# A delta-rule attention and a softplus MLP in one hand-ordered program: one inverse for the first two chunks, its joins split, memsets moved, weights loaded earlier, the order redrawn

## The chip, the core and the metric

The kernel runs on one core of a Trainium2 chip. The time is the device time of one execution in microseconds (us); the figure for a kernel is the median of its runs. The engines are named as in the profile: PE (TensorE) multiplies matrices, with PEld its weight loads; DVE (VectorE) and POOL (GpSimd) work element by element; ACT (ScalarE) evaluates functions and copies; SP (SyncE) issues DMA transfers. Each engine takes its own instructions strictly in the order in which the program lists them.

## The reference, cut to what matters

Four sequences of 768 tokens, 8 heads, 48 features per head. A recurrent state of 48 x 48 per sequence and head is read by the query and corrected by the key; the result, scaled by g, goes through a two-layer MLP with softplus (384 to 2048 to 384) over all 3072 tokens.

```python
k_n = k / (np.linalg.norm(k, axis=-1, keepdims=True) + 1e-06)
for t in range(S):
    readout = np.einsum('bhd,bhde->bhe', q[:, :, t], state)
    y[:, :, t] = g[:, :, t] * readout
    v_old = np.einsum('bhde,bhd->bhe', state, kt)
    state = state + bt[:, :, :, None] * np.einsum('bhd,bhe->bhde', kt, vt - v_old)
...
h = x @ w_in
g = np.maximum(h, 0.0) + np.log1p(np.exp(-np.abs(h)))
return (g @ w_out).astype(np.float32)
```

## The kernel before, in words

**Chunks.** The 768 steps are cut into 12 chunks of 64. Inside a chunk the recurrence becomes a triangular system of 64 x 64 for each of the 32 pairs of sequence and head; between chunks only the state is carried. Chunks are taken in pairs, six in all.

**Front** (`front`, line 468). For one chunk: cast keys (kn) and queries (qn) to f16, transpose them on PE (8 products with the identity, line 485) into kqt by way of PSUM, with copies by ACT and DVE (lines 312 and 314 are the copy helper). The key gram (64 products, lines 522 and 527) gives the strictly triangular blocks kk, the query gram (32 products, line 561) gives mt after a multiplication with the mask (line 571). `norms` squares and sums the keys (lines 418 and 423) and takes the root: on ACT for the first two pairs, on POOL by a power (line 443) afterwards. `lane_beta` makes the factors bl.

**Inverse** (`inverse`, line 584). The blocks are transposed to ln (line 591, on DVE), scaled to nn (line 612), and a forward elimination of 15 steps, each a product (line 622) and a sum (line 629), inverts two 16 x 16 blocks per system, with all systems side by side in the lanes of tt. One pass always works on the shapes of two chunks, whether one chunk or two are in it. In the kernel before there are seven passes: one for chunk 0 on DVE, one for chunk 1 on POOL, and one for each of the other five pairs on POOL. The *join* that follows puts the small inverses together to those of 32 x 32 and 64 x 64: transposes of tt (lines 647 and 663, DVE), copies to f16 (lines 654 and 670, ACT), and three batches of PE products per chunk: xmm (64, line 684), tmm (68, lines 705 and 711) and zmm (34, lines 739 and 742), with evacuations between them, into td and z.

**Chain** (`chain`, line 765). For one chunk, in order: ks (line 786) from the state, w (line 829, or line 799 for chunk 0, which has no state), umm (line 840), u1, zu (line 877), u2, smm and the new state (lines 909 to 926), and beside it the output: qs, ymm (line 939), y times g (line 961), transposes ytr (line 979) into xt. For chunk 0 the products count 64 for umm, and 32 each for zu, smm and ymm, and 6 for ytr.

**Dense** (`dense`, line 998). Jobs of one chunk (the first two and the last two) or two chunks (the others): h = w_in x xt (g1, line 1014), softplus on ACT (line 1028), times w_out (g2, line 1044), evacuation to osb, store (line 1067). The first dense product needs chain 0 and w_in; the job of chunks 2 and 3 needs both of their chains.

**Order.** Nothing runs when it is called: every piece of work is an `Item` with an engine, a planned cost, what it depends on and the buffers it uses. `Plan.run` (line 86) simulates the engines with the planned costs and writes the instructions of each in the order that results; ties are broken by priorities. `_TABLE` (line 1108) gives, by position, the engine (of those that an item allows) and the priority of every item. The planner also has a model of PE's code supply: PE's products are counted in blocks of 128 (`BLOCK`), and a block is taken to arrive `FETCH` after the block before the last was begun.

**Loads.** SP issues k, q, v and g chunk by chunk, two DMAs of 192 KB each, as buffers come free (kf 3, qf 2, vf 4, gf 4). The eight weight loads (w_in and w_out in four parts each) are issued by POOL; each part waits on POOL's queue until a named load of SP has landed: before these are v0, q0, k2, k3 for w_in and q1, v1, g1, g1 for w_out. At the start POOL also issues beta's eight small DMAs, builds the mask, and clears kk, nv and tt (lines 272 and 275).

Of the kernel before, what the change touches and what calls it, by code (L numbers as in the profile page):

```python
# [10 lines left out]
F32 = mybir.dt.float32  # L11
# [34 lines left out]
class Plan:  # L46
# [3 lines left out]
    FETCH = 3.5  # L50
    HOP = 0.08
# [34 lines left out]
    def run(self):  # L86
# [3 lines left out]
        free = {e: 0.0 for e in left}  # L90
        pipe = 0.0
# [3 lines left out]
        while any(left.values()):  # L95
# [64 lines left out]
            if it.dma:  # L160
                free[e] = t0 + it.cost if e == "POOL" else max(t0 + it.cost, pipe - 4.0)
                pipe = max(pipe, t0 + it.cost) + it.dma
                it.end = pipe + 1.9
            elif e == "PE":
# [24 lines left out]
def kernel(  # L189
# [13 lines left out]
    P = 128  # L203
# [67 lines left out]
    def pool0(t):  # L271
        nc.gpsimd.memset(t, 0.0)
# [116 lines left out]
    weights(0, (("v", 0), ("q", 0), ("k", 2), ("k", 3)))  # L389
    weights(1, (("q", 1), ("v", 1), ("g", 1), ("g", 1)))  # L390
# [64 lines left out]
    def lane_beta(cc, nv, nv_it, prio):  # L455
# [9 lines left out]
        it = add("DVE", "lbeta", 0.8, fn, deps=[nv_it], bufs=[nv, nl, bl], prio=prio)  # L465
        return bl, it

    def front(c, kk, prio, late, en_k, en_q, en_kk):
# [9 lines left out]
        for j, x, x_it, pr in ((1, kn[c], kn_it[c], prio + 1), (0, qn[c], qn_it[c], prio + late + 1)):  # L478
# [33 lines left out]
            if j == 1:  # L512
                gk = [Buf(p_d), Buf(p_d)]

                def gram(gk=gk):
# [16 lines left out]
                    "PE", "gramk", 0.75, gram, deps=ev, bufs=gk + kq + [kk], prio=pr, mm=64,  # L532
# [17 lines left out]
            else:  # L550
# [3 lines left out]
                def gram(gm=gm):  # L554
# [9 lines left out]
                    "PE", "gramq", 0.45, gram, deps=its[0] + its[1], bufs=gm + kq + mt[c],  # L564
# [19 lines left out]
    def inverse(cs, kk, kk_it, bl, bl_it, on_dve, clear, prio, prio2):  # L584
# [51 lines left out]
        for j in range(15):  # L636
# [6 lines left out]
        u_all = slice(16 * cls[0], 16 * cls[-1] + 16)  # L643
        part = len(cs) / 2
# [6 lines left out]
        )  # L651
        e2 = add(
            "ACT", "tn", 0.17 + 0.92 * part,
            lambda: nc.scalar.copy(  # L654
                tn.ap[:, u_all], tn32.ap[:, :, u_all].rearrange("p j u -> p u j")
            ),
            deps=[e1], bufs=[tn32, tn], prio=prio2,
# [9 lines left out]
        l3 = add("DVE", "t32", 1.34, ttr, deps=[prev], bufs=[t32, tt], prio=prio2)  # L667
        l4 = add(
# [6 lines left out]

        xp, ep, xs, z = Buf(p_d), Buf(p_d), Buf(r_xs), Buf(r_z)
        e3, e5 = [], []
        for cl in cls:

            def xmm(cl=cl):  # L680
                for u in range(16 * cl, 16 * cl + 16):
# [8 lines left out]
                    "PE", "xmm", 0.53, xmm, deps=[e2], bufs=[kk, tn, xp, xs],  # L690
                    prio=prio2 + cl, mm=64, mode="3232",
# [7 lines left out]
        for cl in cls:  # L699

            def tmm(cl=cl):
# [7 lines left out]
                for u in range(16 * cl, 16 * cl + 16):  # L709
# [12 lines left out]
                    "PE", "tmm", 0.58, tmm, deps=[e4, l4], bufs=[xs, td, ep],  # L722
# [8 lines left out]
        for c in cs:  # L731
# [3 lines left out]
            def zmm(zp=zp, cl=cl):  # L735
# [13 lines left out]
                "PE", "zmm", 0.42, zmm, deps=[td_it], bufs=[kk, td, z, zp],  # L749
# [13 lines left out]
    xts, xt_it = {}, {}  # L763

    def chain(c, pr):
# [39 lines left out]
        else:  # L805

            def vscale():
# [14 lines left out]
                "PE", "ks", 0.37, lambda: with_state(C, wp, lambda b: {}),  # L822
# [13 lines left out]
        def umm(m):  # L836
            for pi in range(H):
# [13 lines left out]
                "PE", "umm", 0.31, lambda m=m: umm(m), deps=[a2[m], td_it],  # L851
# [12 lines left out]
        if not first:  # L864
            c0 = add(
                "PE", "qs", 0.37,
# [7 lines left out]
        def zu(m):  # L874
            for pi in range(H):
# [12 lines left out]
                "PE", "zu", 0.28, lambda m=m: zu(m), deps=[a4[m], z_it],  # L888
# [3 lines left out]
        ]  # L892
        a6 = [
# [6 lines left out]
        if not last:  # L900
# [3 lines left out]
            def smm(kn_=kn[c]):  # L904
# [11 lines left out]
                "PE", "smm", 0.37, smm, deps=a6, bufs=[kn[c]] + u2 + sp_ + s1, prio=pr,  # L916
# [35 lines left out]
        for m in range(2):  # L952
            c1 = add(
                "PE", "ymm", 0.3, lambda m=m: ymm(m), deps=[a6[m]] + mt_it[c],
# [43 lines left out]
    def dense(cs, pm):  # L998
# [8 lines left out]
        for f0 in range(0, NF, nb):  # L1007
            hp, gb = Buf(p_h), Buf(r_ga)

            def g1(f0=f0, hp=hp):  # L1010
# [12 lines left out]
                "PE", "g1", 0.655, g1, deps=[x for c in cs for x in xt_it[c]] + [wl[0][f0 // 4]],  # L1023
# [56 lines left out]
    for cc in range(1, NSS):  # L1080
# [4 lines left out]
        for c in cs:  # L1085
            kk_it += front(c, kk, pf, 70, "POOL", "POOL", ("ACT", "DVE"))
# [125 lines left out]
```

## Time and profile before

| | |
|---|---|
| median of 3 runs | 309.63 us (308.05 to 311.8) |
| profiled execution | 309.16 us |
| its span | 307.5 us |
| PE, DVE, ACT, POOL busy | 236.3, 158.9, 142.9, 142.6 us |
| instructions PE (products) | 6768 |
| DMA | 27.79 MB, of which PE's and the other engines' code 0.94 MB |
| mean granted clock of PE | 0.967 |

The span runs from the first to the last instruction that the profile shows; the time of the execution is a little longer. A row of the views by time gives the start, the length, the engine, the line, the operation and its tiles; "x8" is the number of instructions merged in a row. A row of the view by stretches gives, after the stretch and its length, each engine's busy us with its number of instructions, then PE's granted clock, the share of the DMA engines and GB/s. In the chain that ended last every piece is what the next piece waited for; "issue" is time in which an engine waited for nothing that the profile shows.

### The profile page before, as it was taken

Reading aid. Unit: us, or ns where it says so; the run is one execution under the profiler, and the core shown is the slowest. Engines: PE = TensorE matmul, PEld = TensorE weight load, DVE = VectorE, ACT = ScalarE, POOL = GpSimd, SP = SyncE. Lnnn points to the kernel's source line nnn. Section 1 sums busy time; section 2 is a strip of 40 time slices with the busy share of each in tenths; the row PEclk is TensorE's granted clock in tenths of the full one; section 3 lists DMA queues with packets and bytes.
Section 4 is the critical chain, followed back from the end, with each engine's and each line's share of the span. In section 5 each row is a group of like instructions: output and inputs, shape, how many; then the busy total and the mean of one; then the engine's idle time right before and its main releaser. Section 6 shows DMA issues by size and latency. Waiting matters only on the chain.

```text
span 307.5 us, 14779 instructions
## 1 busy us (share of the span) xinstructions
PE 236.3 (77%) x6768; PEld 155.8 (51%) x6768; DVE 158.9 (52%) x306; ACT 142.9 (46%) x240; POOL 142.6 (46%) x262
## 2 busy tenths in 40 slices
PE   0130183277988997899987999959999899999993
PEld 0120163255756765455664556636555555567761
DVE  1189998442757786854873474645436611152000
ACT  3070086022754656726654674352656516715531
POOL 8916578557138887457761747811087000000000
PEclk9999999999999999969997999987999979999999
DMA  8999439999015979699298430843000111021122
GB/s 115 158 179 173 57 54 191 186 170 152 7 31 100 157 140 158 113 162 148 51 164 147 83 57 15 125 99 79 6 5 15 43 28 30 2 55 28 27 53 51
DMA packets 107711, 27.79 MB, mean 90 GB/s; under 512 B 100865, under 2 KB 107649, under 8 KB 107649
## 3 DMA queue, kind: packets, MB, share of 16 engines
q1 hardware_dynamic: 103680, 23.60, 47.5%
q0 software_dynamic: 3968, 3.25, 7.1%
q8 instruction: 53, 0.87, 1.2%
q14 instruction: 10, 0.07, 0.1%
HBM read 25.26 MB, written 4.72 MB: 98 GB/s over the span
## 4 chain that ended last, share of the span: by engine, by line
PE 61%; DVE 12%; issue 11%; POOL 11%; ACT 4%; POOLq 0%; ACTq 0%
PE h L1014 19%; PE o L1044 18%; PE d L485 3%; POOL tt L629 3%; POOL tmp L622 3%; PE d L684 2%; PE d L786 2%; DVE tt L629 2%; PE d L840 2%; PE d L939 2%; DVE tmp L622 2%; PE d L711 2%; DVE ln L591 2%; PE d L561 2%; PE d L877 2%
## 5 line engine op out<-in xcount | busy, mean ns | idle before, releaser
L1044 PE MATMUL o<-w_out,ga 128*128 128x384 f16 x384 | 77.9, 343 | 3.2 <-issue 1.9
L1028 ACT ACTIVATE ga<-h 128x512 f16<-128x512 f32 x96 | 57.2, 599 | 48.0 <-PE h L1014 45.4
L1014 PE MATMUL h<-xt,w_in 128*128 128x512 f16 (+1 forms) x384 | 74.8, 336 | 1.0 <-issue 1.0
L1044 PEld LDWEIGHTS <-ga 128*128 128x128 f16 x384 | 35.7, 101 | 26.1 <-issue 7.3
L1014 PEld LDWEIGHTS <-w_in 128*128 128x128 f16 x384 | 36.1, 100 | 21.7 <-issue 3.4
L629 POOL TENSOR_TENSOR tt<-tt,tmp 128x30 f32<-128x30 f32 (+7 forms) x90 | 33.8, 375 | 7.0
L622 POOL TENSOR_TENSOR tmp<-nn,tt 128x30 f32<-128x30 f32 (+7 forms) x90 | 32.3, 359 | 6.4
L485 PE MATMUL d<-ident,kn 128*128 128x128 f16 x96 | 9.7, 258 | 30.8 <-POOL kn L314 28.3
L312 ACT ACTIVATE kqt<-d 128x512 f16<-128x512 f16 x26 | 15.0, 596 | 26.2 <-PE d L485 24.5
L314 DVE CAST u<-d 128x384 f16<-128x384 f32 x25 | 13.4, 552 | 26.3 <-PE d L877 18.5
L443 POOL TENSOR_TENSOR nv<-nv,half_c 128x32 f32<-128x32 f32 x4 | 22.0, 5509 | 7.4 <-DVE nv L423 7.4
L485 PEld LDWEIGHTS <-kn 128*128 128x128 f16 x96 | 7.1, 115 | 32.8 <-POOL kn L314 28.7
L571 DVE TENSOR_TENSOR mt<-d,mask 128x512 f16<-128x512 f32 x24 | 15.7, 683 | 9.9 <-PE d L561 9.8
L808 POOL TENSOR_TENSOR vf<-vf,nv 128x768 f32<-128x768 f32 x11 | 16.2, 1476 | 8.2 <-DMA vf<-in_v_dram 5.0
L314 DVE COPY osb<-o 128x384 f32<-128x384 f32 x12 | 6.6, 551 | 22.7 <-PE o L1044 22.7
L961 DVE TENSOR_TENSOR yg<-d,gf 128x384 f16<-128x384 f32 x24 | 12.8, 551 | 10.1 <-PE d L939 10.0
L654 ACT CAST tn<-tn 128x512 f16<-128x512 f32 (+1 forms) x7 | 6.7, 963 | 21.6 <-DVE tn L647 21.6
L314 DVE COPY kqt<-d 128x512 f16<-128x512 f16 x22 | 9.1, 422 | 14.6 <-ACT kqt L312 9.0
L423 DVE TENSOR_REDUCE nv<-ksq 128x16 f32<-128x768 f32 x12 | 11.4, 949 | 9.6 <-POOL nv L275 7.8
L312 ACT ACTIVATE u<-d 128x384 f16<-128x384 f32 x23 | 10.7, 490 | 10.7 <-PE d L840 7.4
L829 DVE TENSOR_TENSOR w<-vf,d 128x384 f16<-128x384 f32 x22 | 11.3, 547 | 8.2 <-PE d L786 4.5
L591 DVE STREAM_TRANSPOSE ln<-kk 128x1024 f16<-128x1024 f16 x7 | 13.3, 1905 | 4.2 <-ACT kk L312 4.0
(89 smaller groups left out, 379.4 us busy)
## 6 DMA issues: line engine op xcount, KB each, us to landing
kf<-in_k_dram SPq DMA_DIRECT2D x24, 192.0 KB, 5.4
vf<-in_v_dram SPq DMA_DIRECT2D x24, 192.0 KB, 5.5
qf<-in_q_dram SPq DMA_DIRECT2D x24, 192.0 KB, 5.5
gf<-in_g_dram SPq DMA_DIRECT2D x24, 192.0 KB, 5.3
out_dram<-osb SPq DMA_DIRECT2D x48, 96.0 KB, 2.3
w_in<-in_moe_w_in_dram POOLq DMA_DIRECT2D x4, 384.0 KB, 8.1
w_out<-in_moe_w_out_dram POOLq DMA_DIRECT2D x4, 384.0 KB, 8.6
beta_l<-in_beta_dram POOLq DMA_DIRECT2D x8, 12.0 KB, 4.5
```

Source lines behind the costliest of these rows:

```text
L312: nc.scalar.activation(o, x, AF.Copy, scale=float(sign))
L314: ENG[en].tensor_copy(o, x)
L443: lambda: nc.gpsimd.tensor_tensor(nv.ap[:, sl], nv.ap[:, sl], half_c[:, sl], ALU.pow),
L485: nc.tensor.transpose(o[:, NP * p + i], x.ap[:, p, 2 * i : 2 * i + 2].rearrange("p h d -> p (h d)"), ident,)
L571: nc.vector.tensor_tensor(o.ap, gm[m].ap.rearrange("p (n t) -> p n t", n=H), mask[:, None, :].broadcast_to([P, H, C]), ALU.mult,)
L591: lambda: nc.vector.transpose(ln.ap, kk.ap[:, 1].rearrange("p u t -> p t u")),
L622: eng.tensor_tensor(t, nn.ap[:, :, j + 1 :, j : j + 1].broadcast_to([P, 2, n, w]), tt.ap[:, :, j : j + 1, 16 : 16 + w].broadcast_to([P, 2, ...
L629: eng.tensor_tensor(rows, rows, t, ALU.add)
L808: nc.gpsimd.tensor_tensor(vf.ap, vf.ap, nv.ap[:, 16 * cl : 16 * cl + 16] .rearrange("p (a h) -> p a h", a=2)[:, :, :, None] .broadcast_to( ...
L1014: nc.tensor.matmul(hp.ap[:, n * b : n * b + n], w_in[:, j, f * P : (f + 1) * P], xt.ap[:, j, t0 : t0 + n], start=(j == 0), stop=(j == 2),)
L1028: lambda hp=hp, o=gb: nc.scalar.activation(o.ap, hp.ap, AF.Softplus),
L1044: nc.tensor.matmul(op.ap[:, :DM], b.ap[:, col + c0 : col + c0 + 128], w_out[:, f, :], start=(f == 0), stop=(f == NF - 1),)
```

## The change

- Chunks 0 and 1 are treated as a pair like the others: one inverse, on DVE. It waits for both chunks' kk and for norms over both.
- The join moves to a function of its own. For the first pair it is done chunk by chunk on the shared transposes: join of chunk 0, chain 0, join of chunk 1. On PE, xmm of chunk 1 is ordered behind zu of chain 0 (`hold`, `behind`).
- kk and nv are no longer cleared; tt is cleared at the start by DVE instead of POOL, and the clear within an inverse is left out for pair 1, which gets the second tt fresh.
- Loads: the order of the first ten becomes k0, k1, q0, v0, q1, k2, k3, g0, v1, g1. The four parts of w_in wait for k0, k0, k1, k1, those of w_out for g0, v1, g1, g1.
- The planner gets other costs for many items, a start time for each engine (`FREE`), a shorter `FETCH`, and an extra `BUSY` for code that is fetched while a weight load is under way.
- `_TABLE` is another one throughout.

The products of the key gram stay as they are; only their planned cost differs.

```diff
-    FETCH = 3.5
-    HOP = 0.08
+    FETCH = 3.2
+    BUSY = 2.3
+    HOP = 0.06
+    FREE = {"PE": 1.0, "ACT": 2.4, "DVE": 5.5, "POOL": 6.8, "SP": 0.8}
...
-                    arrive.append(end + self.FETCH)
+                    arrive.append(end + self.FETCH + (self.BUSY if end < wide else 0.0))
...
-    r_kk = ring("kk", 2, [P, 2, U, HC], F16, init=pool0)
-    r_nv = ring("nv", 3, [P, 32], F32, init=lambda t: nc.gpsimd.memset(t, 1.0))
-    r_t = ring("tt", 2, [P, 2, 16, 48], F32, init=pool0)
+    r_kk = ring("kk", 2, [P, 2, U, HC], F16)
+    r_nv = ring("nv", 3, [P, 32], F32)
+    r_t = ring("tt", 2, [P, 2, 16, 48], F32, init=lambda t: nc.vector.memset(t, 0.0))
...
-        ("k", k, r_k, 0), ("k", k, r_k, 1), ("v", v, r_v, 0), ("q", q, r_q, 0),
-        ("g", g, r_g, 0), ("k", k, r_k, 2), ("k", k, r_k, 3), ("q", q, r_q, 1),
+        ("k", k, r_k, 0), ("k", k, r_k, 1), ("q", q, r_q, 0), ("v", v, r_v, 0),
+        ("q", q, r_q, 1), ("k", k, r_k, 2), ("k", k, r_k, 3), ("g", g, r_g, 0),
...
-    weights(0, (("v", 0), ("q", 0), ("k", 2), ("k", 3)))
-    weights(1, (("q", 1), ("v", 1), ("g", 1), ("g", 1)))
+    weights(0, (("k", 0), ("k", 0), ("k", 1), ("k", 1)))
+    weights(1, (("g", 0), ("v", 1), ("g", 1), ("g", 1)))
...
-                    "PE", "gramk", 0.75, gram, deps=ev, bufs=gk + kq + [kk], prio=pr, mm=64,
+                    "PE", "gramk", 0.51, gram, deps=ev, bufs=gk + kq + [kk], prio=pr, mm=64,
...
+        l3 = add("DVE", "t32", 1.34, ttr, deps=[prev], bufs=[t32, tt], prio=prio2)
+        for grp in [[c] for c in cs] if apart else [cs]:
+            plan.tag = grp[0]
+            join(
+                grp, kk, tn32, e1, t32, l3, tn, td, xs, z,
+                prio2 + apart * (grp[0] - cs[0]), hold.get(grp[0] - 1, ()),
+            )
+            if apart and grp[0] == cs[0]:
+                chain(grp[0], -300)
+
+    def join(cs, kk, tn32, e1, t32, l3, tn, td, xs, z, prio2, behind):
...
-                    "PE", "xmm", 0.53, xmm, deps=[e2], bufs=[kk, tn, xp, xs],
-                    prio=prio2 + cl, mm=64, mode="3232",
+                    "PE", "xmm", 0.47, xmm, deps=[e2], bufs=[kk, tn, xp, xs],
+                    prio=prio2 + cl, mm=64, mode="3232", order=behind,
...
+        hold[c] = a5
...
-    for c in range(2):
-        nv, kk = Buf(r_nv), Buf(r_kk)
-        kk_it = front(c, kk, -400 + 20 * c, 12, "DVE", "POOL", ("ACT", "DVE"))
-        nv_it, _ = norms([c], nv, -405 + 20 * c, True)
-        bl, bl_it = lane_beta(0, nv, nv_it, -395 + 20 * c)
-        nv_of[c] = (nv, nv_it)
-        inverse([c], kk, kk_it, bl, bl_it, c == 0, False, -450 + 60 * c, -430 + 60 * c)
-    for cc in range(1, NSS):
+    for cc in range(NSS):
...
-        inverse(cs, kk, kk_it, bl, bl_it, False, True, pf + 5, pf + 60)
+        inverse(cs, kk, kk_it, bl, bl_it, cc == 0, cc > 1, pf + 5, pf + 60 if cc else -430, 0 if cc else 200)
...
-    for c in range(2 * NSS):
-        chain(c, 100 * c - (300 if c == 0 else 100))
+    for c in range(1, 2 * NSS):
+        chain(c, 100 * c - 100)
...
-S-3237 S-3039 S-361 S1100 S-2853 S-242 S-370 S501 S-739 S-2146 S-3210 S-973 S182 S-1859 S508 S1283
+S-4579 S-2995 S-2904 S1894 S-2679 S-170 S-2166 S954 S2708 S-4953 S-4843 S-1370 S-1003 S-4019
...
```

More of the change, by code (lines that the diff above doesn't have):

```diff
@@ L89, in run @@
             left[it.eng].append(it)
-        free = {e: 0.0 for e in left}
-        pipe = 0.0
+        free = dict(self.FREE)
+        pipe = wide = 0.0
         mode = None
@@ L163, in run @@
                 it.end = pipe + 1.9
+                wide = it.end if e == "POOL" else wide
             elif e == "PE":
@@ L667, in inverse @@
         l3 = add("DVE", "t32", 1.34, ttr, deps=[prev], bufs=[t32, tt], prio=prio2)
+        for grp in [[c] for c in cs] if apart else [cs]:
[7 more added lines that the diff above has]
+    def join(cs, kk, tn32, e1, t32, l3, tn, td, xs, z, prio2, behind):
+        cls = [c % 2 for c in cs]
+        u_all = slice(16 * cls[0], 16 * cls[-1] + 16)
+        part = len(cs) / 2
+        e2 = add(
+            "ACT", "tn", 0.17 + 0.92 * part,
+            lambda: nc.scalar.copy(
+                tn.ap[:, u_all], tn32.ap[:, :, u_all].rearrange("p j u -> p u j")
+            ),
+            deps=[e1], bufs=[tn32, tn], prio=prio2,
+        )
         l4 = add(
@@ L1085 @@
         for c in cs:
-            kk_it += front(c, kk, pf, 70, "POOL", "POOL", ("ACT", "DVE"))
+            kk_it += front(
+                c, kk, pf, 70 if cc else 20, "POOL" if c else "DVE", "POOL", ("ACT", "DVE")
+            )
         nv_it, root = norms(cs, nv, pf - 2, cc < 2)
```

188 lines of the change are left out of this document (89 added, 99 removed).

## The prediction

> **What bounds the kernel now.** I read the page first, then the chain that ended last, then the stretches before and after the first dense product, then the instructions of each engine in the first 75 us.
>
> ```profile
> span 307.5 us, 14779 instructions
> PE 236.3 (77%) x6768; PEld 155.8 (51%) x6768; DVE 158.9 (52%) x306; ACT 142.9 (46%) x240; POOL 142.6 (46%) x262
> ```
>
> Two stretches with different limits hide in that 77%. The view by stretches, cut where the first dense product starts, parts them (length; busy us and instructions of PE, its weight loads, DVE, ACT, POOL; granted clock, DMA share, GB/s):
>
> ```profile
> 0.00:72.90 72.90, 23.27 (x1019) 18.36 (x1020) 44.97 (x97) 22.68 (x41) 48.45 (x102) 1.00 1.02 142
> 72.90:307.50 234.60, 213.00 (x5750) 137.47 (x5750) 113.94 (x209) 120.23 (x199) 94.12 (x161) 0.96 0.42 74
> ```
>
> For 72.9 us PE is busy 23.27 us (32%); then it is busy 213.0 of 234.6 us (91%). So the end is set by **when the first dense product can start**, plus PE's work from there. The chain, in order of time, says what the first 72.9 us wait for:
>
> ```profile
> 6.76 3.54 POOL kk L272 x2
> 10.48 2.63 POOL tt L272 x2
> 13.17 0.83 POOL kn L314
> 14.05 1.05 PE d L485 x8
> ...
> 20.10 1.80 DVE ln L591
> ...
> 37.29 0.04 DVE tn L647
> ...
> 52.09 3.08 issue
> ...
> 57.37 4.26 issue
> ...
> 65.39 1.35 issue
> ...
> 70.12 1.99 issue
> 72.90 2.62 PE h L1014 x12
> ```
>
> Three pieces: to 13.17 POOL clears buffers and only then casts the first keys; to 37.29 VectorE prepares and inverts chunk 0; from there to 72.90 joins and chains run with long "issue" gaps, in which PE waits for nothing that the profile shows. Cut at the ends of those gaps, the stretches (PE alone) show what they are:
>
> ```profile
> 48.69:55.16 6.47, 2.03 (x128) 1.00 1.37 190
> 55.16:61.63 6.47, 2.19 (x128) 1.00 1.26 186
> 61.63:66.73 5.10, 3.06 (x128) 1.00 1.03 169
> 66.73:72.11 5.38, 3.39 (x130) 1.00 1.06 149
> ```
>
> PE stops after every 128 products, that is 256 instructions with their weight loads. That is a block of its code arriving late: 23.42 us for four blocks, 5.1 to 6.5 us each, slowest where the DMA share (last but one column) is highest. Later, with dense products between, the pace is bounded by 177.1 us for 4867 products, 4.66 us a block, at half the DMA share:
>
> ```profile
> 72.90:250.00 177.10, 160.37 (x4867) 103.16 (x4868) 104.12 (x190) 95.03 (x155) 94.12 (x161) 0.94 0.50 87
> ```
>
> [...]
>
> **The change, step by step.** "Two products per triangle" has no counterpart in the diff: the key gram (lines 522 and 527) has two products per block in the kernel shown, and only its planned cost changes. No product is added or removed, so I expect 6768 again; this part is worth nothing. The planned costs, FETCH, BUSY and FREE cost no instruction either: with the redrawn table they set the order alone.
>
> *Step 1, to the first elimination step.* The diff removes the POOL memsets of kk and nv and moves those of tt to VectorE, and the first casts may go to another engine.
>
> ```profile
> 6.10 0.84 ACT L418 ACTIVATE ksq<-kf 128x768 f32<-128x768 f32 x1 [3.79 <-DMA kf<-in_k_dram]
> 0.81 3.42 SPq L344 DMA_DIRECT2D kf<-in_k_dram  x4
> kf<-in_k_dram SPq DMA_DIRECT2D x24, 192.0 KB, 5.4
> 2.18 0.45 DVE L238 MEMSET qn<- 128x128 uint32 x3
> 20.02 1.88 DVE L591 STREAM_TRANSPOSE ln<-kk 128x1024 f16<-128x1024 f16 x1
> 21.93 0.76 DVE L612 TENSOR_TENSOR nn<-ln,bl 128x256 f32<-128x256 f16 x2
> 24.41 0.16 DVE L622 TENSOR_TENSOR tmp<-nn,tt 128x30 f32<-128x30 f32 x1
> ```
>
> k0 is there at 6.10, but its cast waits until 13.17. VectorE ends its own preparation at 2.63; the two tt memsets take it 2 to 3.2 us (POOL's took 2.63 for both, 0.86 ns an element; VectorE's elimination, below, takes 1.04 ns), so to 5.8 at most: under k0's load, at no cost. If k0 came earlier they would cost up to 3 us. The joint inverse now also waits for k1: its issues end at 4.23, and it lands between 7.8 (k0's 3.6 us after its last issue) and 9.6 (the median of 5.4); I take 8.7. From cast to first step: cast 0.83, eight transposes 1.05, two copies of 0.6 (rows at step 3), gram and negated copy estimated at 0.7 each, ln 1.88, nn 0.76 and some 0.3 of hops, 7.4 us clean; before took 11.24 (13.17 to 24.41). With the reductions and norms of two chunks in VectorE's queue I take 8.3: steps start at **17.0** (16.1 to 20.8) instead of 24.41.
>
> *Step 2, the elimination.* Before: 24.41 to 37.29, 12.9 us, beside POOL's inverse of chunk 1.
>
> ```profile
> 26.57 0.33 DVE L629 TENSOR_TENSOR tt<-tt,tmp 128x78 f32<-128x78 f32 x1
> 35.22 0.42 POOL L629 TENSOR_TENSOR tt<-tt,tmp 128x120 f32<-128x120 f32 x1
> 36.06 0.24 DVE L629 TENSOR_TENSOR tt<-tt,tmp 128x78 f32<-128x78 f32 x1
> 37.06 0.19 DVE L629 TENSOR_TENSOR tt<-tt,tmp 128x30 f32<-128x30 f32 x1
> ```
>
> The same 78 elements take 0.33 with POOL busy and 0.24 at 36.06, when POOL's last step before a pause has ended (35.64). Both chunks share one pass at the same shapes, so chunk 1's inverse costs VectorE nothing more and leaves POOL altogether. From the last two rows, 0.16 us plus 1.04 ns an element, the 30 operations (2720 elements) with 0.03 between would take 8.5 us alone. Yet VectorE is in order, and what the table puts between the steps (pair 1's reductions, copies and ln, an estimate of up to 7 us, ln's 1.88 among them) delays them. Ends: 8.5 and 20; I take 12.5, near the old duration: the steps end at **29.5** instead of 37.29.
>
> *Step 3, join and chain of chunk 0, to the first dense product.* Before this took 35.6 us, because VectorE's backlog (casts, reductions, norms) stood ahead of chain 0 and the join of chunk 1, arriving separately, was planned into the middle of it. Now the join of chunk 1 may go on PE only behind chain 0's zu products.
>
> ```profile
> L312 ACT ACTIVATE kqt<-d 128x512 f16<-128x512 f16 x6 | 3.4, 599 | 5.0 <-PE d L485 5.0
> L654 ACT CAST tn<-tn 128x256 f16<-128x256 f32 x2 | 1.3, 630 | 15.9 <-DVE tn L647 15.9
> L312 ACT ACTIVATE xs<-d 128x256 f16<-128x256 f32 x2 | 0.8, 384 | 2.3 <-PE d L684 2.3
> 63.36 0.58 PE d L909 x25
> ```
>
> Bare: 1.0 for the transpose (half of ln's elements), seven PE batches near 0.6, copies of 0.63 and 0.38, six more steps of VectorE or ACT of 0.4 to 0.6 each like these, hops: 10.5 us. The code is 166 products of the join and 166 of the chain, 2.6 blocks: at 4.66 to 6.47 us 12 to 17. Part of it is fetched while PE waits for the inverse; I take 13.5. If the table puts pair 1's key fronts (144 products) and the query grams (80) here as well, 1.75 blocks or 8 to 11 us more. First dense product at **43** (37 to 54) instead of 72.9.
>
> *Step 4, loads.* w_in moves ahead of q0, v0, q1, k2 and k3.
>
> ```profile
> q0 software_dynamic: 3968, 3.25, 7.1%
> L371 POOL DMA_DIRECT2D w_in<-in_moe_w_in_dram x4: 741/762/786, 13.9 to 51.4; - x4
> 12.45 6.71 SPq L344 DMA_DIRECT2D kf<-in_k_dram  x4
> 53.21 1.20 POOL L612 TENSOR_TENSOR nn<-ln,bl 128x256 f32<-128x256 f16 x2 [1.04 <-DVE ln L591]
> ```
>
> All eight weight loads take 7.1% of 307.5 us, 21.8 us of all DMA engines, so four take 10.9. Issued at 7 to 11 us they can delay what is behind by that; k0 and k1 are ahead of them. k3 was issued by 19.2, so it was there at 24.6 (5.4 later) and is now there at 25 to 35. Its consumer is POOL's first pass, now pair 1, which started at 53.21; with k3 at 30 and 5 us of front it starts near 35. POOL is free until then: the cover is 18 us. POOL queues two of the weight issues (0.76 each) ahead of k1's cast at worst: 1.5 us, inside step 1's upper end. In return PE's code in step 3 no longer meets w_in, whose last issue was at 51.4.
>
> *Step 5, the rest.* From the first dense product on there were 234.6 us. By 43 PE will have run some 650 products instead of 1019 (224 in the fronts of pair 0, 332 in step 3, 94 of others); the other 369, at 22.8 ns (23.27 / 1019), add 8.4. POOL has five passes instead of six and runs ahead, so the one place where PE starved late should shrink:
>
> ```profile
> 200.00:210.00 10.00, 6.41 (x174) 3.81 (x170) 3.92 (x7) 4.11 (x5) 1.47 (x1) 0.75 0.37 75
> ```
>
> I take 3 of those 3.6 idle us back. **Sum**: 43 + 234.6 + 8.4 - 3 = 283.0 us of span. The profiled execution took 309.16 with its span of 307.5, 1.66 outside: 284.7, and the median of the runs shown, 309.63, lies 0.47 above it: **285 us**. Every other row is redrawn as well; bounds of step 3 alone give 279 to 296, and PE at 89% or 93% instead of 91% is 5 us either way: 276 to 294 for this case.
>
> **The rivals.** *A thin start.* Dense [0] and [1] come early, but dense [2,3] needs pair 1, and PE runs dry. Before, 254.3 us lay between the start of pair 1's pass (53.21) and the end of the span. If ln of pair 1 stands behind VectorE's steps and joins, and k3 comes late, the pass starts at 42 and the span ends at 296: 298. For it: the 35.6 us of step 3, most of them VectorE's backlog. Against: POOL's 18 us of cover.
>
> *Only the memsets pay.* If loads and VectorE's backlog keep everything past chunk 0 where it was, the end moves by the POOL memsets alone, from 6.76 to 13.11 in the chain, 6.4 us: 303. Against: chunk 1 no longer needs a POOL pass.
>
> *PE's own idle shrinks more.* The planner now counts late code where weights load. Half of the 21.6 idle us after the first dense product gone, and all else as forecast: 274 or so.
>
> *Slower: code supply sets the whole pace.* The loads are now earlier and PE's small products denser. After the first dense product 6118 products, 47.8 blocks, remain; (307.5 - 43) / 47.8 = 5.53 us a block is the point from which the change loses. At the mean of the four blocks above, 5.86, it ends at 323: 325 us. For it: those four blocks. Against: 4.66 us was reached over 177 us at a DMA share of 0.5, and the bytes to load are the same.
>
> **How the numbers follow.** A measurement of this kernel can tell about 1%, 3.1 us, from no change. Forecast 0.54; thin start 0.17; only the memsets 0.10; less idle 0.11; slower 0.08. Faster by over 1% (under 306.5): the first four, less a part of the third whose gain is small: 0.86. Slower: 0.08; within 1%: 0.06. The range goes from 270, below the case with less idle, to 302, past the thin start and short of the two cases that barely gain or lose.
>
> **What would show it.** Right: first kn cast near 6.2 and not on POOL behind memsets; one VectorE pass, ending near 29.5; first dense product near 43; pair 1's POOL pass near 35; 6768 products; about 240 us from the first dense product to the end, PE 89 to 93% busy there. Step 2 is wrong if the pass ends past 33, step 3 if blocks in it still take 6 us, step 4 if pair 1's pass starts past 42. The whole is wrong if the first dense product moves 30 us and the end doesn't: then PE's stretch has grown, and its idle time will name the reason.

## The result, and the profile after

The changed kernel takes 291.34 us (median of 4 runs, 287.1 to 295.53) where the kernel before takes 310.31 on the same chip; the ratio is 0.9313 (95% interval 0.9174 to 0.9452). The ratios here and below leave out executions that took over 1.5% more than the fastest of their kernel, so they are not quotients of the medians. Forecast were 285, with 270 to 302 around it. The sign and the range held; the median came out 6.3 us above the forecast.

The execution profiled first took 295.53 us, more than the other three, and in it the first queries landed late; so the same kernel was run and profiled once more (six runs, median 291.59, 289.47 to 297.13; before on that chip 309.96; ratio 0.9519, 0.9351 to 0.9687), and the second profile is the one read below. It is of the fastest of those six executions, so its span lies some 2 us under what the median would give. The pages of the two begin so, the first with

```profile
span 293.7 us, 14732 instructions
PE 236.0 (80%) x6768; PEld 156.6 (53%) x6768; DVE 154.3 (53%) x305; ACT 142.4 (49%) x236; POOL 121.0 (41%) x218
```

and the second with a span of 287.8 us, 19.7 less than before. PE has its 6768 products as expected, 44 instructions have left POOL, and its busy time has fallen from 142.6 to 121.0 us.

The view by stretches of the second profile, cut where the first elimination pass ends and where the first dense product starts:

```profile
0.00:49.76 49.76, 18.61 (x801) 15.07 (x802) 36.13 (x88) 16.88 (x28) 18.36 (x33) 1.00 1.12 161
49.76:287.80 238.04, 216.17 (x5969) 141.11 (x5968) 116.53 (x218) 125.68 (x208) 102.65 (x185) 0.96 0.47 83
27.71:49.76 22.05, 13.10 (x617) 10.65 (x617) 14.30 (x29) 11.20 (x19) 6.03 (x8) 1.00 1.05 157
```

The first dense product starts 23.1 us earlier than before (49.76, not 72.9), yet 3.4 us of that are given back behind it (238.04, not 234.60). A second cut says more. The transpose tn of pair 1 on VectorE is the moment at which that pair's elimination pass is over and its join begins. The stretches up to it and from it, before:

```profile
0.00:81.26 81.26, 31.52 (x1177) 24.59 (x1178) 49.62 (x107) 26.55 (x49) 51.12 (x107) 1.00 0.98 136
81.26:307.50 226.24, 204.76 (x5593) 131.25 (x5591) 109.29 (x201) 116.35 (x193) 91.45 (x155) 0.95 0.41 74
```

and in the second profile after:

```profile
0.00:67.52 67.52, 34.66 (x1163) 26.19 (x1164) 44.14 (x101) 25.75 (x44) 31.85 (x66) 1.00 1.10 161
67.52:287.80 220.28, 200.12 (x5605) 129.99 (x5604) 108.52 (x206) 116.81 (x193) 89.16 (x153) 0.96 0.43 77
```

Up to that moment PE has run nearly the same work, 1177 and 1163 products; what remains, some 5600 products, takes 226.2 and 220.3 us. So 13.7 of the 19.7 us come from the moment of tn, and 6.0 from the rest, of which 4.6 are PE's own busy time (204.76 to 200.12) for as many products. Single profiles do not settle how much of the 6.0 is the change's: in the third, fourth and seventh experiment below, which leave the work behind tn as it is in the changed kernel, the rest takes 221.5 to 223.3 us, and in the first, which has the order of before, 224.03. The fourth experiment's row:

```profile
66.53:289.70 223.17, 203.49 (x5605) 131.29 (x5604) 108.50 (x206) 116.83 (x193) 89.41 (x153) 0.95 0.42 76
```

Where the 13.7 come from is read off POOL's and VectorE's instructions. Before, pair 1's pass (begun at 53.21) is broken in the middle:

```profile
64.00 0.82 POOL L314 CAST kn<-kf 128x768 f16<-128x768 f32 x1 [5.51 <-PE d L909]
...
69.70 0.82 POOL L314 CAST qn<-qf 128x768 f16<-128x768 f32 x1
...
74.20 0.25 POOL L629 TENSOR_TENSOR tt<-tt,tmp 128x30 f32<-128x30 f32 x1
```

```profile
78.20 0.55 DVE L961 TENSOR_TENSOR yg<-d,gf 128x384 f16<-128x384 f32 x1
...
81.26 1.11 DVE L647 STREAM_TRANSPOSE tn<-tt 128x512 f32<-128x512 f32 x1
```

A key cast of a later chunk stands between its steps and waits 5.51 us for PE; two casts add 1.64; and when the last step has ended at 74.45, tn stands on VectorE behind chain 1's work until 81.26. In the second profile after, nothing is between:

```profile
51.68 1.19 POOL L612 TENSOR_TENSOR nn<-ln,bl 128x256 f32<-128x256 f16 x2 [3.31 <-DVE ln L591]
...
66.03 0.25 POOL L629 TENSOR_TENSOR tt<-tt,tmp 128x30 f32<-128x30 f32 x1
```

```profile
67.52 1.04 DVE L646 STREAM_TRANSPOSE tn<-tt 128x512 f32<-128x512 f32 x1
```

The pass starts 1.5 us earlier (51.68), takes 14.6 us instead of 21.2, and its result waits 1.2 us for VectorE instead of 6.8: 1.53 + 6.64 + 5.57 = 13.74.

One sentence of the description above has to be corrected: the weight loads do not wait on POOL's queue until a named load has landed; the name only places them in the planner's order. The trace of the first experiment below shows it. It has the loads of the kernel before, where the first part of w_in is named after v0:

```profile
4.25 2.72 SPq L344 DMA_DIRECT2D vf<-in_v_dram  x2
7.51 0.78 POOL L371 DMA_DIRECT2D w_in<-in_moe_w_in_dram  x1
```

v0's second issue ends at 6.97, and no load of v in the first 40 us of that run landed in under 5.2 us; the weights are issued at 7.51 all the same.

### The profile page after: what moved, and what is told of

The parts are those of the page before. It is cut to its first block, busy times and chain, and to the rows that moved or that the text cites. A ratio compares the mean times of both kernels' runs of the same rounds, so it can differ in the third digit from the quotient of the medians.

```text
span 293.7 us, 14732 instructions
## 1 busy us (share of the span) xinstructions
PE 236.0 (80%) x6768; PEld 156.6 (53%) x6768; DVE 154.3 (53%) x305; ACT 142.4 (49%) x236; POOL 121.0 (41%) x218
## 4 chain that ended last, share of the span: by engine, by line
PE 76%; issue 9%; DVE 6%; DMA 3%; ACT 2%; SPq 2%; POOL 0%; POOLq 0%
PE h L1027 24%; PE o L1057 23%; PE d L485 4%; DMA qf<-in_q_dram 3%; PE d L798 3%; PE d L952 3%; PE d L852 3%; PE d L696 3%; PE d L889 2%; PE d L723 2%; DVE tmp L622 2%; SPq L344 2%; PE d L922 2%; PE d L992 2%; DVE tt L629 2%
## 5 line engine op out<-in xcount | busy, mean ns | idle before, releaser
L629 POOL TENSOR_TENSOR tt<-tt,tmp 128x30 f32<-128x30 f32 (+7 forms) x75 | 28.5, 380 | 5.9
L622 POOL TENSOR_TENSOR tmp<-nn,tt 128x30 f32<-128x30 f32 (+7 forms) x75 | 27.0, 360 | 5.5
L312 ACT ACTIVATE u<-d 128x384 f16<-128x384 f32 x29 | 13.7, 489 | 20.8 <-PE d L889 13.2
L696 PE MATMUL d<-tn,kk 16*32 16x16 f16 x768 | 7.9, 171 | 16.0 <-ACT tn L676 14.0
L312 ACT ACTIVATE kqt<-d 128x512 f16<-128x512 f16 x18 | 10.7, 596 | 20.7 <-PE d L485 19.7
L612 POOL TENSOR_TENSOR nn<-ln,bl 128x256 f32<-128x256 f16 x10 | 6.0, 619 | 34.6 <-DVE ln L591 34.6
L314 DVE CAST u<-d 128x384 f16<-128x384 f32 x19 | 10.4, 555 | 18.6 <-PE d L852 8.2
L696 PEld LDWEIGHTS <-kk 16*32 16x32 f16 x768 | 7.0, 89 | 17.6 <-issue 17.1
L974 DVE TENSOR_TENSOR yg<-d,gf 128x384 f16<-128x384 f32 x24 | 12.5, 548 | 4.7 <-PE d L952 4.6
L312 ACT ACTIVATE osb<-o 128x384 f32<-128x384 f32 x14 | 6.9, 493 | 15.0 <-PE o L1057 14.8
L683 ACT CAST td<-t 128x1024 f16<-128x1024 f32 (+1 forms) x7 | 12.0, 1712 | 4.1 <-DVE t L655 4.0
```

What stands on the lines that cost most here:

```text
L312: nc.scalar.activation(o, x, AF.Copy, scale=float(sign))
L314: ENG[en].tensor_copy(o, x)
L622: eng.tensor_tensor(t, nn.ap[:, :, j + 1 :, j : j + 1].broadcast_to([P, 2, n, w]), tt.ap[:, :, j : j + 1, 16 : 16 + w].broadcast_to([P, 2, ...
L629: eng.tensor_tensor(rows, rows, t, ALU.add)
L696: nc.tensor.matmul(uv(xp.ap)[QUAD[qd], u], kk.ap[r, 1, u, :], tn.ap[r, u, :])
```

## The experiments

Two theories were set against each other. By the first, the **front**, the time follows the first dense product, as the forecast's sum has it. By the second, the **thin start** (a rival in the prediction), early dense work only uses up what lies ready, and the time follows pair 1's pass. No experiment leaves out or changes a part of the computation.

**1 and 2. How much is it the memsets, and the weights?** Both edit the kernel before; its table, its two inverses and its order stay. In the first the memsets of kk, nv and tt go to VectorE.

```diff
-        nc.gpsimd.memset(t, 0.0)
+        nc.vector.memset(t, 0.0)
...
-    r_nv = ring("nv", 3, [P, 32], F32, init=lambda t: nc.gpsimd.memset(t, 1.0))
+    r_nv = ring("nv", 3, [P, 32], F32, init=lambda t: nc.vector.memset(t, 1.0))
```

> The kernel before with one part of the change: kk, nv and tt are cleared at the start by VectorE instead of GpSimd; the order of everything else is that of before. Theory 'front' (the end moves with the first dense product, which moves with the start): the first key cast goes from 13.17 to about 6.8 us, VectorE's memsets (2.7 us for tt, 2 to 3.5 for kk) end by 9, the elimination ends near 31 to 33 instead of 37.3, the first dense product comes near 67 instead of 72.9, and the time is 303 to 305 us (ratio 0.98). Rival 'order' (only the redrawn order gains; an earlier start is given back in PE's long stretch or in the joins): first dense product near 72, time within 1% of before.

Measured: 300.89 us (299.16 to 305.9) against 309.92, ratio 0.9687 (0.9607 to 0.9767): 9 us, more than expected. The first key cast no longer waits for POOL's memsets, and what follows moves with it:

```profile
6.75 0.82 POOL L314 CAST kn<-kf 128x768 f16<-128x768 f32 x1
```

```profile
67.20:300.60 233.40, 213.57 (x5756) 137.50 (x5750) 113.29 (x209) 120.16 (x199) 95.14 (x165) 0.96 0.40 74
...
76.57:300.60 224.03, 204.23 (x5592) 130.67 (x5589) 108.64 (x201) 116.16 (x192) 91.06 (x155) 0.96 0.41 75
```

The cast moves 6.4 us, the first dense product 5.7, tn of pair 1 4.7 (to 76.57), and the profiled span 6.9. By the medians the memsets alone are thus worth about half of the change, by the spans about a third. The second adds the early weights: all four parts of w_in go out in one go at the place of the first.

```diff
+        elif not w_in_done:
+            w_in_done.append(1)
+            for i in range(4):
+                fs = slice(FF // 4 * i, FF // 4 * (i + 1))
+                nc.gpsimd.dma_start(
...
-                    lambda dst=dst, src=src: nc.gpsimd.dma_start(out=dst, in_=src),
+                    lambda dst=dst, src=src: issue(which, dst, src),
```

> The kernel before with the memsets on VectorE as in the other run and, besides, all four parts of w_in issued on GpSimd right behind the first key cast; everything else in the order of before. Theory 'front' with code supply as the limit of the join: w_in no longer meets PE's code at 47 to 52 us, the blocks in the join take nearer 4.7 than 6.5 us, the first dense product comes 3 to 4 us before that of the run with memsets alone, time 299 to 302 us. Rival 'loads': w_in ahead of q0, v0, k2 and k3 makes these late by up to 10 us, which stalls the queues that wait for them: first dense product no earlier than in the other run or later, time 303 us or more.

Measured: 303.91 us (303.02 to 305.0), ratio 0.9805 (0.9747 to 0.9862). The first dense product comes 1.2 us earlier than in the first experiment (66.0), tn of pair 1 as well (75.37), and the time is 3 us longer. What remains after tn takes 227.93 instead of 224.03 us, with PE busy 207.10 instead of 204.23 at a granted clock of 0.95 instead of 0.96. Earlier weights alone did not pay here; why PE's time grew isn't settled.

**3 and 4. Two suspects in the changed kernel.** One holds w_in back until q0's cast; the other puts VectorE's copy of q0's transposes behind the norms, since in the first profile that copy, waiting for the late q0, held up the pass:

```profile
5.93 9.96 DMA qf<-in_q_dram
```

```profile
18.60 0.42 DVE L314 COPY kqt<-d 128x512 f16<-128x512 f16 x1 [2.62 <-ACT kqt L312]
```

```diff
+                release() if (name, c) == ("q", 0) else None,
```

> The changed kernel, but all four parts of w_in are issued on GpSimd behind the cast of q0 (which waits for q0), not at 6.6 and 10.2 us; the order on every engine is otherwise the same. In the changed kernel q0 took until 15.9 us, and VectorE's copy of q0's transposes stood ahead of the last norm operations and held the elimination back by 2.6 us. Theory 'w_in delays q0': q0 is there near 12, steps start near 18.3 instead of 20.9, first dense product 2 to 3 us earlier, time 285 to 287 us. Rival 'earlier weights are what pays': w_in then loads during the join (at 31 to 45 us), code blocks there get slower, first dense product no earlier, time same or up to 3 us more.

```diff
+        if cc == 0:
+            kqt_it[0][1].order.append(bl_it)
```

> The changed kernel with one thing moved: on VectorE the copy of q0's transposes comes behind the last norm operations of the first pair, not ahead of them. Theory 'front': the norm operations no longer wait for q0, steps start near 18.3 instead of 20.9, and all that follows comes 2.6 us earlier: first dense product near 50.8, time 285 to 286 us where the changed kernel takes 288 to 289. Rival 'the join is bound by loads and code, not by the elimination's end': first dense product stays at 53, time the same.

Measured: 292.01 us (287.9 to 296.3) with w_in held back, 292.31 (289.79 to 293.23; ratio 0.9416, 0.9346 to 0.9486) with the copy moved; the changed kernel has 291.34 and 291.59. First dense product at 50.8 and 49.5, tn of pair 1 at 67.8 and 66.5. Neither moves the time. q0 was in time in both, as in the second profile of the changed kernel, where the elimination starts at 18.03 and not at 20.91. The 2.6 us of the first profile are that execution's, not the kernel's.

**5 and 6. Without the tables.** The planner then takes its default engines and priorities, in the changed kernel and in the one before. What differs between the two is the structure: the joint inverse, the split joins, the memsets, the loads, the planned costs.

```diff
-    plan.use(_TABLE)
```

> The changed kernel without its table: every item keeps the engine and the priority that the code gives it, and the planner orders by these. Theory 'structure' (joint inverse, memsets off GpSimd, chunk 1's join behind chain 0 bring the first dense product forward, whatever the table): it starts before 62 us, and the run is at least 12 us faster than the kernel before without its table. Rival 'order' (the gain is the table's): first dense product at 65 us or later, and less than 6 us between the two runs without tables.

> The kernel before without its table, by the code's own priorities. Theory 'structure': first dense product at 70 us or later (its memsets on GpSimd and its two separate inverses are still there), time 310 to 325 us. Rival 'order': within 6 us of the changed kernel without its table.

Measured: 307.03 us (306.13 to 308.58), ratio 0.9876 (0.9805 to 0.9946), after; 320.26 (318.73 to 322.75), ratio 1.0303 (1.0223 to 1.0384), before. The structure is worth 13.2 us without tables, as expected of it, and the new table 15.4 on top of it. In the changed kernel without its table the first dense product starts at 57.8 and tn of pair 1 at 71.49. The kernel before without its table missed its expectation in the place that matters: its first dense product starts at 50.0, as early as in the changed kernel, and it is the slowest but one of all. Its stretches from the first dense product and from tn of pair 1:

```profile
50.00:320.80 270.80, 231.66 (x6108) 148.47 (x6107) 112.52 (x210) 124.64 (x210) 123.50 (x224) 0.88 0.40 72
...
79.11:320.80 241.69, 208.18 (x5589) 132.49 (x5586) 101.38 (x193) 113.15 (x190) 98.09 (x166) 0.89 0.39 72
```

and from tn of pair 1 in the changed kernel without its table:

```profile
71.49:306.70 235.21, 206.68 (x5600) 134.04 (x5574) 103.00 (x196) 114.42 (x190) 97.53 (x164) 0.92 0.42 77
```

An early first dense product gained nothing: 23 us early at the front, 36 us more behind it. The front theory was in doubt from here. But behind tn, too, these two orders take 241.69 and 235.21 us, not the 220 to 228 of the runs with a table: the moment of tn fixes the end only as long as the order behind it stays. POOL did chunk 1's pass from 42.3 on, and pair 1's only from 62.0; tn came at 79.11.

**7. Pair 1's pass held up, first try.** Eight memsets of tt on POOL ahead of pair 1's pass, about 11 us of its work.

```diff
+            if cs[0] == 2:
+                for _ in range(8):
+                    nc.gpsimd.memset(tt.ap, 0.0)
```

> The changed kernel with eight more memsets of tt on GpSimd (1.37 us each, 11 us in all) ahead of pair 1's inverse; tt is the same afterwards. Pair 1's pass, which started at 55.3 us, then starts near 60 to 66 us. Theory 'front' (PE has enough other work; the pass has slack): time within 3 us of the changed kernel, first dense product unmoved. Rival 'thin start' (the pass of pair 1 sets the end, as the prediction priced it, one for one): 8 to 11 us more, 297 to 300 us.

Measured: 294.06 us (291.72 to 294.75), ratio 0.9434 (0.9351 to 0.9516). The memsets fell into POOL's idle time from 35.89 to 47.3, the pass started at 51.99 and tn came at 69.21 instead of 67.52: 1.7 us late, and 2.5 us more. That does not tell the theories apart.

**8. What slows VectorE's pass?** The casts of q1, k2 and k3 go from POOL to ACT.

```diff
-            lambda en, f=f, o=o: copy(en, o.ap[:, :, :, :D], f.ap),
+            lambda en, f=f, o=o: copy(
+                "ACT" if (name, c) in (("q", 1), ("k", 2), ("k", 3)) else en, o.ap[:, :, :, :D], f.ap
+            ),
```

> The changed kernel with three casts (q1, k2, k3) on ScalarE instead of GpSimd. In the changed kernel three of VectorE's thirty elimination operations took 0.78 to 0.87 us instead of 0.24 to 0.29, each while one of these casts ran on GpSimd. Theory 'VectorE and GpSimd exclude each other': all thirty are then at 0.19 to 0.30 us, and the pass takes 8.6 us instead of 10.3. Rival 'something else slows these three' (the loads that land then): they stay, pass near 10.

Measured: one run, 290.68 us. In the changed kernel, a step of the pass that meets a cast on POOL is long (the second profile, POOL and then VectorE):

```profile
23.70 0.95 POOL L314 CAST qn<-qf 128x768 f16<-128x768 f32 x1 [11.36 <-DMA qf<-in_q_dram]
26.79 0.85 POOL L314 CAST kn<-kf 128x768 f16<-128x768 f32 x1 [2.14 <-DMA kf<-in_k_dram]
```

```profile
24.00 0.77 DVE L622 TENSOR_TENSOR tmp<-nn,tt 128x110 f32<-128x110 f32 x1
...
26.98 0.69 DVE L629 TENSOR_TENSOR tt<-tt,tmp 128x30 f32<-128x30 f32 x1
```

Both begin inside a cast and end within 0.12 us of its end. With the casts on ACT the group of two 110-element products takes 0.274 us each, the mean of a group row of that run:

```profile
L624 DVE TENSOR_TENSOR tmp<-nn,tt 128x110 f32<-128x110 f32 x2 | 0.5, 274 | 0.1
```

No step is over 0.3 us, and the pass takes 8.65 us (17.90 to 26.55). That is the 8.6 that the theory gave. The two steps above, 0.77 and 0.69 us beside a cast, take 0.27 and 0.19 here: 0.5 us lost for each cast met; what holds the step up no row shows. The time doesn't follow the pass: tn of pair 1 comes 1.4 us earlier (66.14), and one run of 290.68 can't be told from 291.59.

**9. The changed kernel again.** The kernel is the changed one, for the second profile.

> The changed kernel once more, as the base for the others of this call and for a profile in which q0 lands in time. In its first profile q0 landed at 15.9 us and the elimination started at 20.9; two other runs with the same order started it at 17.9. Theory 'front': first dense product between 48 and 51 us instead of 53.4, the stretch from there to the end 232 to 241 us as in every run of this order, time 287 to 291 us. Rival: the late q0 belongs to the kernel, first dense product at 53 again.

Measured: as given with the result. The first dense product (49.76) and the stretch behind it (238.04) lie where theory 'front' had them; the median, 291.59, just above.

**10. The memsets back on POOL, in the changed kernel.**

```diff
-    r_kk = ring("kk", 2, [P, 2, U, HC], F16)
-    r_nv = ring("nv", 3, [P, 32], F32)
-    r_t = ring("tt", 2, [P, 2, 16, 48], F32, init=lambda t: nc.vector.memset(t, 0.0))
+    r_kk = ring("kk", 2, [P, 2, U, HC], F16, init=pool0)
+    r_nv = ring("nv", 3, [P, 32], F32, init=lambda t: nc.gpsimd.memset(t, 1.0))
+    r_t = ring("tt", 2, [P, 2, 16, 48], F32, init=pool0)
```

> The changed kernel with kk, nv and tt cleared by GpSimd at the start again, as before the change; the order of everything else is the same. GpSimd then casts k1 and issues w_in only from about 13.2 us instead of 9.5 and 6.6. Theory 'front': elimination and first dense product 3 to 4 us later, time 3 to 4 us more (291 to 295 us); together with the 5.7 us that the same memsets were worth in the kernel before, this says how much of the gain they are. Rival: w_in issued later frees the loads for q0, v0 and k2, and the time is the same.

Measured: 294.89 us (289.88 to 301.34): 3.3 more than the changed kernel, within the scatter of its runs. The profiled spans differ by 5.2 us (293.0 and 287.8): ln of pair 0 is 5.8 us later (19.73), the first dense product 5.8 (55.6), tn of pair 1 4.7 (72.2). The trace moves in step, at a mean granted clock of 0.969 against 0.970; the median alone would not show it. Here the memsets are worth about a quarter of the 19.7 us of span.

**11. Pair 1's pass held up, second try.** Now 36 memsets stand inside the pass, of the half of nn that is filled right after them, where no idle time can take them.

```diff
+            if cs[0] == 2 and b == 0:
+                for _ in range(36):
+                    nc.gpsimd.memset(nn.ap[:, 1], 0.0)
```

> The changed kernel with 36 small memsets of a buffer that is overwritten next, in the middle of pair 1's inverse on GpSimd, behind its wait for ln: the pass then ends 9 to 12 us later (the earlier try put its memsets where GpSimd was idle, and moved the pass by about 2 us). Theory 'front' (PE has other work until then): 0 to 4 us more. Rival 'thin start' (one for one, as the prediction priced it): 9 to 12 us more, 297 to 301 us.

Measured: 303.31 us (10 runs, 301.71 to 306.75), ratio 0.9929 (0.9841 to 1.0017). POOL, then VectorE, then the stretches:

```profile
52.83 13.49 POOL L620 MEMSET nn<- 128x256 f32 x36
```

```profile
80.20 1.05 DVE L649 STREAM_TRANSPOSE tn<-tt 128x512 f32<-128x512 f32 x1 [12.29 <-POOL tt L632]
```

```profile
80.20:301.70 221.50, 201.19 (x5549) 129.77 (x5548) 108.61 (x205) 116.80 (x192) 90.27 (x153) 0.93 0.42 76
50.80:70.00 19.20, 16.18 (x413) 11.32 (x402) 7.85 (x13) 8.96 (x16) 15.02 (x46) 0.97 0.94 140
70.00:80.00 10.00, 1.22 (x19) 0.55 (x18) 0.00 (x0) 0.00 (x0) 8.28 (x23) 0.50 0.00 0
```

The first dense product stays at 50.8; tn comes 12.7 us later (80.20 instead of 67.52), the span ends 13.9 later, the median 11.7. PE works off the ready dense work until 70 and then stands: 1.22 us of 10. PE's list of waits from 60 to 92 has one long one:

```profile
PE d L925 <- DVE mt L571: 10.7, 1, 10.7
```

mt is right behind tn in VectorE's order:

```profile
81.18 0.65 DVE L571 TENSOR_TENSOR mt<-d,mask 128x512 f16<-128x512 f32 x1
```

**One for one: the thin start holds, the front theory falls.** What PE waits for in that halt is not the join of pair 1 itself but mt, held up because VectorE stands at tn; an order with tn behind mt was not run.

**12. Pair 1's key grams behind chain 0.** If the front theory were right, taking pair 1's key fronts out of PE's way would pay.

```diff
-                    mode="6432",
+                    mode="6432", order=xt_it[0] if c in (2, 3) else (),
```

> The changed kernel with the key grams of chunks 2 and 3 placed on PE behind chain 0's output; the planner moves some neighbours with them (738 products instead of 800 ahead of the first dense product). Theory 'products times code blocks' (step 3 is as long as its products are many): first dense product 2 to 3 us earlier than in the changed kernel. Theory 'front' adds: time 2 to 3 us less. Rival 'only the supply over the whole counts': first dense product earlier, time the same or more, because pair 1's pass starts later.

Measured: 321.43 us (317.5 to 324.94), ratio 1.0474 (1.0242 to 1.0705). The first dense product came at 54.9, not earlier; pair 1's ln and pass went far back:

```profile
69.53 1.90 DVE L591 STREAM_TRANSPOSE ln<-kk 128x1024 f16<-128x1024 f16 x1
...
100.62 1.04 DVE L646 STREAM_TRANSPOSE tn<-tt 128x512 f32<-128x512 f32 x1 [2.71 <-POOL tt L629]
```

```profile
100.62:323.20 222.58, 192.29 (x5216) 122.75 (x5215) 96.21 (x177) 106.09 (x173) 76.88 (x140) 0.85 0.37 63
...
100.00:120.00 20.00, 10.00 (x539) 8.35 (x539) 7.99 (x13) 7.76 (x11) 17.48 (x30) 0.50 0.77 106
```

tn is 33.1 us later than in the changed kernel and the end 35.4 (the medians differ by 29.8; this profile is of the slowest of four executions). That the rest takes 222.58 us is in part chance: 389 products fewer are left than in the changed kernel, at a clock of 0.85 instead of 0.96. Nor did fewer products make the way to the first dense product shorter:

```profile
30.53:54.90 24.37, 12.36 (x555) 10.35 (x554) 13.71 (x26) 11.58 (x20) 3.35 (x5) 1.00 1.08 157
```

That is 2.3 us more than in the changed kernel for 62 products fewer, which theory 'products times code blocks' had wrong.

## Why the prediction was right, and where it was not

Over the runs with a table, from before to the last experiment, tn of pair 1, at the end of its pass, starts between 66 and 101 us and the rest takes 220 to 228; the first dense product lies between 48 and 73, and what follows it takes 233 to 268. So in this order the time is set by **when pair 1's pass is over and tn can start**, not by when the first dense product starts. The forecast named that mechanism as a rival and took the other. That it still came near is in part luck: the change moves both moments, and errors of its sum offset each other. By its steps:

- *Step 1, the first elimination step: right.* 18.03 (17.0 forecast). The tt memsets lie on VectorE from 2.89 to 5.84, before k0 is there, and it then waits 0.39 us for k0: they cost nothing; the first key cast moved to VectorE, at 6.23 (6.2 forecast).
- *Step 2, the pass: right in its bounds, a little long.* 18.03 to 27.71 is 9.7 us, not 12.5. The 8.5 us worked out for a pass alone was measured as 8.65 in the eighth experiment. Pair 1's work, which was to stretch it, came later; casts on POOL stretched it by about 1.
- *Step 3, to the first dense product: mis-sized.* 22.05 us, not 13.5. 617 products stand in it, the first dense one among them, not 332. Besides 300 of chunk 0's join and chain the table puts 144 of pair 1's fronts here, as the upper case named there has it, and 172 of chunk 1. Of these 132 are its join, which stands behind chain 0's zu but still ahead of the first dense product. 617 are 4.82 blocks; 22.05 / 4.82 is 4.57 us a block, a little under the 4.66 to 6.47 that were used, so here the count was the error and not the price. The price is not fixed, though: in the twelfth experiment 555 products, 4.34 blocks, took 24.37 us, 5.6 a block. With 1.0 us late from step 1 and 2.8 early from step 2, its 8.55 make the 6.76 by which the first dense product misses 43. The chain of the second profile shows the halts between, and the stretches from the end of one to the end of the next have 128 products each:

```profile
33.14 1.31 issue
...
37.96 1.60 issue
...
42.50 2.16 issue
...
47.80 1.14 issue
...
49.76 1.39 PE h L1027 x6
```

```profile
34.45:39.55 5.10, 3.14 (x128) 2.62 (x128) 2.61 (x4) 2.17 (x4) 0.47 (x1) 1.00 1.11 170
39.55:44.64 5.09, 2.94 (x128) 2.45 (x128) 2.61 (x7) 3.05 (x6) 0.00 (x0) 1.00 0.93 155
44.64:48.92 4.28, 3.05 (x128) 2.16 (x128) 3.52 (x9) 0.87 (x2) 2.99 (x5) 1.00 0.87 152
```

  The four halts are 6.2 of the 22.05 us; the rest is work and waits between engines. That such a halt is code arriving late fits the traces of before (five halts from 47.10 to 72.11) and of the first profile (four from 36.69 to 52.53): in each a packet of the instruction queue q8 lands 1.2 to 1.7 us before PE goes on. The second profile has 53 of these packets, `q8 instruction: 53, 0.87, 1.3%`, for 6768 products, one for 127.7.

- *Step 4, pair 1's pass: wrong.* It starts at 51.68, not near 35. Neither k3 nor POOL is at fault: k3's cast runs at 29.17, and POOL stands idle for 3.31 us before the pass. ln waits for VectorE's evacuation of kk, which ends just before it:

```profile
47.78 1.88 DVE L316 TENSOR_SCALAR kk<-d 128x512 f16<-128x512 f32 x3
49.69 1.90 DVE L591 STREAM_TRANSPOSE ln<-kk 128x1024 f16<-128x1024 f16 x1
```

  That evacuation waits for pair 1's key grams, which PE reaches only in the last third of step 3's 617 products: they run from 42.1 to 46.4, with the halt of 2.16 us above in their middle. Before, too, ln waited for an evacuation of kk, and started at 51.22. What the change moved was the pass's own length and its wait for VectorE, 6.64 and 5.57 us, and the prediction had seen neither, because it looked at the start of the pass and not at its end.
- *Step 5, the rest: right in number, by terms that offset each other.* 240.0 us forecast, 238.04 measured, PE busy 90.8% of it. By the first dense product PE had run 801 products, not some 650, so less was added behind it than the 8.4 us forecast (PE's busy time there grew by 3.17); and the 3 us of idle time to be won back did not come. So 287.8 is 283.0, plus 6.76 of the first dense product, less 1.96.
- *Thin start: the right mechanism at the wrong price.* It set 254.3 us from the start of pair 1's pass to the end, as before. Measured: 287.8 - 51.68 = 236.1. The 18.2 between are the 6.64 and 5.57 above and the 5.96 of the rest.
- *Only the memsets pay: refuted, though they pay more than priced.* In the kernel before they are worth 9 us by the medians and 6.9 by the spans, where 6.4 were priced.
- *PE's own idle shrinks more: no.* 238.04 - 216.17 are 21.9 idle us behind the first dense product; before it was 21.6.
- *Code supply sets the pace: refuted.* From the first dense product on, 5969 products are 46.6 blocks in 238.04 us, 5.1 us a block, with PE busy 91%: PE's work, not its code, fills that time.

What stays open: why the early weights cost time in the second experiment, whether the cast that left the middle of the pass would cost its 6.64 us again if it alone were put back, what makes the rest longer without the tables, and how the 15.4 us of the table part into single edits of the order. No version faster than the changed kernel by more than the scatter was found.

## What to carry to other kernels

Look for the moment behind which the remaining time is constant over several variants that keep the order behind it: that moment, not the first product of the big stage, is what a change has to bring forward. For a helper pass on another engine read start, end and the first use of its result; here what paid was that foreign instructions left the middle of the pass and the queue behind it, while its start hardly moved. Test the marker by delaying it alone, at a place where no idle time can take up the delay.

## What the runs showed of the hardware

The granted clock of PE was 1.00 in the first 48 us of every profile but the seventh experiment's, where no row gives it; in the second profile of the changed kernel PE was busy 18.61 of the first 49.76 us. While PE stood in the eleventh experiment it was 0.50 (70 to 80 us, PE busy 1.22 us); in the twelfth it was 0.50 over 100 to 120, with PE busy half of the time, and its mean over the last 222.58 us was 0.85. Why it was 1.00 beside the idle time at the start and 0.50 in these two stretches isn't shown by any run. A memset of 128 x 1536 f32 (tt) takes 1.34 us on VectorE (changed kernel); two took 2.69 on POOL (before): for tt the gain lies in the queue that they leave, not in a faster engine. A memset of kk takes 0.91 us on VectorE (first experiment) and 1.80 on POOL (before).
